# adaLN, multi-query attention and a bilinear FFN on one core: side products on one PSUM bank, one row half per key tile, and heads' outputs through DRAM

## The chip, the core and the metric

The kernel runs on one core of a Trainium2 chip. Time is device time in microseconds of one execution. The median before is 1765.92 us (three runs, 1764.85 to 1766.06). The engines are called PE (TensorE, matmuls), DVE (VectorE), ACT (ScalarE), POOL (GpSimd) and SP (SyncE, which issues the DMAs).

## The reference

```python
# x: 2048 x 512 (f32), 32 heads of 16, one key and one value head, F = 1792
mod = (silu(c) @ w_mod).reshape(1, 6, 1, 512)          # sa, ca, ga, sb, cb, gb
h = layernorm(x) * (1 + ca) + sa
q, k, v = h @ wq, h @ wk, h @ wv                       # k, v: 2048 x 16, shared by all heads
p = softmax(q k^T / 4)
x = x + ga * ((p v) @ wo)
h = layernorm(x) * (1 + cb) + sb
x = x + gb * (((h @ w_gate) * (h @ w_up)) @ w_down)
```

## The kernel before

**Units and key tiles.** The 2048 queries are cut into `NQ` = 8 blocks of 256, the 32 heads into four groups of 8: 32 units `u`, with `b, g = divmod(u, 4)`. A unit holds 16 key tiles of 128 keys, 512 key tiles in all. A key tile has two steps (`p` = 0, 1). Each operand is split into f16 halves (high and low part), so that a product has three terms; queries and keys are laid out so that one matmul over 48 to 50 rows holds all the terms of a score.

**The two row halves.** Scores need 50 of PE's 128 rows. So they are paired: one matmul on rows 0 to 63 (`a` = 0) and one on rows 64 to 127 (`a` = 1) run side by side.

- `max_mm` (L548): a matmul `mx` of queries by 512 keys, and a DVE reduction (L559) to the row maximum. Maxima run ahead of the scores by `LEAD` = 38 steps. Each unit's maxima are transposed (L571) and written into two more rows of the queries, so that the score comes out with its maximum taken off.
- `qk_exp` (L589): a score `sc` of 128 keys by 512 queries, and the exponential on ACT (L596) into a tile `P`.
- `pv` (L598): the previous key tile's four `P` parts against values, four column groups side by side in f32 (eight matmul records), into one bank. Values carry a column of ones, so that sums come along.

After a unit `pv_out` (L605) evacuates the bank and `normalise` (L618) divides by the sums through two small DRAM round trips; its `mult` leaves the heads' output as two f16 parts in `och`, of which four stand in SBUF.

**Side products.** Everything else that is dense is a `Group`: n products of 512 columns that accumulate in one bank, and an evacuation. `q_proj` has 12 products in a group, `wo_work` 12 (two groups for each block), gate and up 12 each (seven pairs for each block, each product as two of 256 columns), down 42 (two groups for each block). A block of queries has 24 + 168 + 84 = 276 products. `duo` (L483) takes two groups at a time, in the banks `misc` and `spare`: in its first turn group 0 has the upper rows and group 1 the lower ones, in its second turn the other way round, so that a bank is never written by both halves at once. While no duo runs, `spare` serves as a third bank for scores.

PSUM has eight banks: three `mx`, two `sc`, `misc`, `spare` and `pv`.

**The order.** The instructions of each engine stand in the order in which the Python loop writes them. In a key tile the loop writes for each step two pairs of `mx` and `sc`; between the steps come side products (as many as `pace` finds due, `burst`), after the second step the previous tile's `pv`. Evacuations are put into `posts` and written a step later. Block b's side work starts in block b + 1, at step 16 of its first unit. The last block's own side work comes after attention: `cover`, `run`.

**Weights.** From step 0 of attention on, `side_step` writes one item at a time: first every weight slice is loaded and squared on ACT (L873) and summed on POOL (L875) for bounds (`ABS_GAP` steps apart), then loaded again and split in f16 parts on POOL (`SPLIT_GAP` apart). `LAG` items lie between load and use.

Of the kernel before, what the change touches and what calls it, by code (L numbers as in the profile page):

```python
# [21 lines left out]
NB = 4  # L22
# [7 lines left out]
LEAD = 38  # L30
ABS_GAP = 1.5
SPLIT_GAP = 2.0
GC = 448
LAG = 3
NSC = 2
NMX = 3
PRE_FILL = 1000.0
# [19 lines left out]
def adaln_mqa_glu_kernel(ctx: ExitStack, tc: tile.TileContext, x_in, wq_in, wk_in, wv_in, wo_in,  # L57
# [43 lines left out]
    wqs = work.tile([128, KC, 128], F32, name="wqs", tag="xl", bufs=4)  # L101
# [3 lines left out]
    for i in range(6, 8):  # L105
        xts.append(work.tile([128, 2, D], F32, name="P", tag="P", bufs=4))
    for i in range(8):
        if i == 2:
# [5 lines left out]
           for tag, n in (("n2", 2), ("ev", 3), ("P", 4), ("P", 4))]  # L114
    for w in wq0:
        nc.gpsimd.memset(w, 0.0)
    wqst = [work.tile([128, D], F32, name="wqst", tag=("gf", "xl")[k // 2], bufs=(2, 4)[k // 2]) for k in range(KC)]
# [177 lines left out]
    mrow = work.tile([128, 256], F32, name="modrow", tag="xl", bufs=4)  # L295
# [181 lines left out]
    def product(p, g, i, j, rows, start, stop):  # L477
        left, right = g.op(i) if g.parts == 1 else g.op(i, j)
        w = 512 // g.parts
        nc.tensor.matmul(p[:, j * w:(j + 1) * w], left[rows], right[rows], start=start and j == 0,  # L480
                         stop=stop and j == g.parts - 1, skip_group_check=g.parts > 1)
# [68 lines left out]
    def max_mm(u, i, a):  # L550
# [3 lines left out]
        if i == 0 and a == 0:  # L554
            mparts[u] = work.tile([128, 2, 2, 4, 4], F32, name="mpart")
# [30 lines left out]
    och = {}  # L586
    rsum = {}

    def qk_exp(u, kt, p, a):  # L589
        s = sst[u % 3]  # L590
        if (u, kt, p) not in ptl:
            ptl[u, kt, p] = work.tile([128, 2, D], F32, name="P", tag="P", bufs=4)
        t = ps_sc()
        nc.tensor.matmul(t, kst[64 * a:64 * a + 50, kt * 128:(kt + 1) * 128],  # L594
                         s[64 * a:64 * a + 50, p, :], start=True, stop=True)
        nc.scalar.activation(ptl[u, kt, p][:, a, :], t, AF.Exp)  # L596

    def pv(u, kt):  # L598
        if kt == 0:
            pvb[u] = psum.tile([128, 512], F32, name="pv", tag="pv", bufs=1)  # L600
        for j in range(4):
            p, a = divmod(j, 2)
            nc.tensor.matmul(pvb[u][32 * j:32 * j + 32, :], vst[:, kt, :], ptl[u, kt, p][:, a, :],  # L603
# [14 lines left out]
    def normalise(u):  # L618
# [13 lines left out]
        def mult():  # L632
# [3 lines left out]
            h = work.tile([128, 2, QT], F16, name="och", tag="och", bufs=4)  # L636
# [17 lines left out]
    xls = {}  # L654
# [3 lines left out]
    def load_x(b, t):  # L658
        xl = work.tile([128, D], F32, name="xl", tag="xl", bufs=4)
        r0 = b * QT + t * 128  # L660
        nc.sync.dma_start(xl, x_rows[r0:r0 + 128, :])
        xls[b, t] = xl

    def wo_work(b):
# [13 lines left out]
        def fin(t):  # L678
            def f(p):
                if b < NQ - 1:  # L680
                    x1 = work.tile([128, D], F32, name="x1", tag="x1", bufs=4)
                else:
                    x1 = work.tile([128, D], F32, name="x1p", tag="P", bufs=4)
                nc.vector.scalar_tensor_tensor(x1, p, sca[:, 7:8], xls[b, t], op0=OP.mult, op1=OP.add)  # L684
                x1s[b, t] = x1
# [22 lines left out]
                if t == 1:  # L708
                    for j, d in enumerate((4, 6)):
                        after(d, n2f[b, j])  # L710
                    if tick[0] is not None:
                        turned.extend([tick[0] + 8 + 2 * j, *it[1:], b] for j, it in enumerate(ln2_work(b, ps_mx)))
# [9 lines left out]
    def ln2_work(b, bank=None):  # L722
# [3 lines left out]
        def tr(j):  # L726
            def f():
                if j == 0:
                    h2s[b] = big.tile([128, 2, KC, QT], F16, name="h2T", tag="h2T", bufs=2)
# [100 lines left out]
    def late_weights():  # L830
# [11 lines left out]
        def m1():  # L842
            st["row"] = work.tile([128, D], F32, name="modrow", tag="xl", bufs=4)
# [20 lines left out]
        def stage(n):  # L864
            t = work.tile([128, D], F32, name="wsl", tag="xl", bufs=4)
# [137 lines left out]
    later = {}  # L1003
    mstep = [0]

    def drain_posts():
        todo = posts[:]
        posts.clear()
        if tick[0] is not None:
            tick[0] += 1  # L1010
            todo += timers.pop(tick[0], [])
# [8 lines left out]

    def max_half(a):
        u, i = divmod(mstep[0], NSTEP)
        if a == 1:
            mstep[0] += 1
        if u >= NU:
            return
        max_mm(u, i, a)
        if a == 1 and u + 1 < NU and i == (QPRE if u else QPRE0):
            load_q(u + 1)
        if i == NSTEP - 1 and a == 1:  # L1030
            max_fin(u)
            (_, f, g), = max_rows(u)
            later[mstep[0] + 1] = (f, g)

    def late_max():
        for at in [m for m in later if m <= mstep[0]]:
            f, g = later.pop(at)
            f()
            posts.append(g)

    fill = deque()
    cur = {"gen": None, "left": 0, "swapped": -9, "wait": 0, "one": False}
    credit = [0.0]

    END = NU * NSTEP

    def pace(step):

        n, most = cur["left"], 0.0
        if n:
            most = n / max((cur["due"] - step) / 2, 1.0)
        for _, kind, what, due in fill:
            n += 4.0 if kind == "solo" else what.n if kind == "one" else 2 * what[0].n
            kept = RESERVE / PAIR if due > (NU - 1) * NSTEP else 0.0
            most = max(most, (n - kept) / max((due - step) / 2, 1.0))
        return most

    def open_gate(step):  # L1060
        if not fill or (fill[0][1] == "one" and step < cur["wait"]):
            return False
        if fill[0][1] == "duo" and NU * NSTEP - step < 2 * -(-fill[0][2][0].n // BURST) + 2:
            return False
        gate = fill[0][0]
        if len(gate) > 2 and ready[0] < gate[2]:
            return False
        if len(gate) > 3 and step < ln_end.get(gate[3], END) + LN_WAIT:
            return False
        if gate[0] is None:  # L1070
            gate[0] = step + gate[1]
        return gate[0] <= step

    def fill_gap(step):


        if cur["gen"] is None:
            if not open_gate(step):
                return
            _, kind, what, due = fill.popleft()  # L1080
            if kind == "solo":
                _, f, post = what
                credit[0] -= 4.0
                f()
                if post:
                    posts.append(post)
                return
            if kind == "one":
                cur.update(gen=plain(what), left=what.n, turn=what.n, second=True, due=due, swapped=-9, one=True)
            else:  # L1090
                begin(step, what, due)
        if cur["one"]:
            burst(step, max(1, min(int(credit[0]), cur["left"], MOST_ONE)))
            return
        turn = cur["turn"]
        parts = max(-(-turn // BURST), min(round(turn / max(credit[0], 1.0)), turn // LEAST), 1)
        n = -(-turn // parts)
        if not cur["second"]:
            n = max(n, -(-cur["turn"] // max((NU * NSTEP - 2 - step) // 2, 1)))
        burst(step, n)  # L1100

    def begin(step, two, due, tags=("misc", "spare")):
        cur.update(gen=duo(*two, tags=tags), left=2 * two[0].n, turn=two[0].n, second=False, due=due, swapped=-9,
                   one=False)

    def burst(step, n):
        for _ in range(n):
            swap = next(cur["gen"], None)
            credit[0] -= 1.0
            cur["left"] -= 1  # L1110
            cur["turn"] -= 1
# [173 lines left out]
```

## Time and profile before

| | us |
|---|---|
| median of the runs | 1765.92 |
| the profiled execution | 1765.83 |
| its span | 1764.0 |
| PE busy | 1700.3 |
| DVE busy | 1416.7 |
| ACT busy | 1252.3 |
| POOL busy | 472.9 |

The granted clock of PE was 0.99 on average. In the rows of the profile a group reads: line, engine, operation, tiles written and read, shapes, count, then busy time, mean ns of one, and idle time of the engine just before it with what ended most of that. In a timeline a row is: start, time until the last of the merged instructions ends, engine, line, operation, tiles, shapes, count and idle time. A window's row is: the window, its length, busy time and count of PE, PEld (weight loads), DVE, ACT and POOL, the granted clock, the DMA share and GB/s; where it was asked for one line's instructions, it holds their engine alone. PE's matmuls are pipelined and their ends are modelled: what a matmul costs is read from one start to the next.

### The profile page before, as it was taken

Reading aid. Unit: us, or ns where it says so; the run is one execution under the profiler, and the core shown is the slowest. Engines: PE = TensorE matmul, PEld = TensorE weight load, DVE = VectorE, ACT = ScalarE, POOL = GpSimd, SP = SyncE. Lnnn points to the kernel's source line nnn. Section 1 sums busy time; section 2 is a strip of 40 time slices with the busy share of each in tenths; the row PEclk is TensorE's granted clock in tenths of the full one; section 3 lists DMA queues with packets and bytes.
Section 4 is the critical chain, followed back from the end, with each engine's and each line's share of the span. In section 5 each row is a group of like instructions: output and inputs, shape, how many; then the busy total and the mean of one; then the engine's idle time right before and its main releaser. Section 6 shows DMA issues by size and latency. Waiting matters only on the chain.

```text
span 1764.0 us, 38680 instructions
## 1 busy us (share of the span) xinstructions
PE 1700.3 (96%) x15571; PEld 699.7 (40%) x15571; DVE 1416.7 (80%) x2367; ACT 1252.3 (71%) x2343; POOL 472.9 (27%) x711
## 2 busy tenths in 40 slices
PE   6999999889999999999999999999999999999999
PEld 3322222234433344334443344334443444334556
DVE  7788888878988889889888988889888888886021
ACT  3468887767777777777777777777777777777710
POOL 5724343788912011111112011201112011201112
PEclk9899999989999999999999999999999999999999
DMA  5223321322200000000000000000000000000000
GB/s 198 89 74 103 94 87 52 99 83 78 78 25 12 24 10 8 23 10 25 12 25 13 24 12 10 20 10 24 13 25 12 25 13 11 19 23 7 8 31 13
DMA packets 68735, 67.15 MB, mean 38 GB/s; under 512 B 24518, under 2 KB 53322, under 8 KB 68556
## 3 DMA queue, kind: packets, MB, share of 16 engines
q1 hardware_dynamic: 66972, 64.35, 11.9%
q8 instruction: 122, 2.00, 0.5%
q14 instruction: 57, 0.47, 0.1%
q10 hardware_dynamic: 1584, 0.33, 0.1%
HBM read 51.25 MB, written 8.92 MB: 34 GB/s over the span
## 4 chain that ended last, share of the span: by engine, by line
PE 82%; ACT 9%; DVE 4%; POOL 3%; issue 2%; SPq 0%; DMA 0%; ACTq 0%; DVEq 0%; POOLq 0%
PE pv L603 27%; PE misc L480 26%; PE mx L557 13%; PE sc L594 13%; ACT P L596 6%; DVE mpart L559 2%; ACT ev L609 1%; ACT hf L742 1%; PE misc L257 1%; PE mx L733 1%; DVE x L684 1%; ACT qf L524 0%; POOL ry L189 0%; DVE bs L223 0%; PE mxt L571 0%
## 5 line engine op out<-in xcount | busy, mean ns | idle before, releaser
L559 DVE TENSOR_REDUCE mpart<-mx 128x1 f32<-128x512 f32 x2048 | 1306.8, 683 | 193.0 <-PE sc L594 163.4
L596 ACT ACTIVATE P<-sc 128x512 f32<-128x512 f32 x2048 | 1108.4, 595 | 329.6 <-PE sc L594 326.1
L557 PE MATMUL mx<-kst,sst 48*128 48x512 f16 x2048 | 657.8, 383 | 11.4 <-DVE mpart L559 7.4
L594 PE MATMUL sc<-sst,kst 50*128 50x512 f16 x2048 | 638.7, 380 | 30.1 <-ACT P L596 18.0
L603 PE MATMUL pv<-P,vst 128*32 128x512 f32 x4096 | 548.3, 608 | 0.0
L557 PEld LDWEIGHTS <-sst 48*128 48x128 f16 x2048 | 163.3, 94 | 528.5 <-issue 484.1
L480 PE MATMUL misc<-h2T,wg 64*128 64x256 f16 (+1 forms) x2520 | 319.5, 269 | 1.3 <-DVE h2T L746 1.1
L480 PE MATMUL misc<-h2T,wu 64*128 64x256 f16 (+1 forms) x2520 | 319.2, 269 | 0.2 <-DVE x L804 0.2
L480 PEld LDWEIGHTS <-wu 64*128 64x128 f16 (+1 forms) x2520 | 237.0, 94 | 41.3
L480 PEld LDWEIGHTS <-wg 64*128 64x128 f16 (+1 forms) x2520 | 236.3, 94 | 38.4 <-issue 5.9
L594 PEld LDWEIGHTS <-kst 50*128 50x128 f16 x2048 | 149.7, 94 | 93.0 <-issue 69.9
L790 POOL TENSOR_SCALAR glu<-gf 128x512 f16<-128x512 f32 x56 | 34.7, 620 | 522.8 <-DVE gf L788 522.8
L480 PE MATMUL misc<-wd,glu 64*128 64x512 f16 (+1 forms) x1176 | 166.6, 376 | 0.4
L603 PEld LDWEIGHTS pv<-P,vst 128*32 128x32 f32 x4096 | 80.8, 108 | 146.1 <-issue 142.1
L635 POOL TENSOR_TENSOR oc<-oc,rr 128x256 f32<-128x256 f32 x31 | 22.6, 730 | 350.3 <-DMA sst<-qd 324.7
L480 PEld LDWEIGHTS <-glu 64*128 64x128 f16 (+1 forms) x1176 | 66.5, 94 | 81.3 <-issue 7.1
L788 DVE TENSOR_TENSOR gf<-misc,g 128x512 f32<-128x512 f32 x56 | 38.2, 683 | 71.9 <-ACT g L782 40.3
L875 POOL TENSOR_TENSOR kwb<-kwb,wsl 128x448 f32<-128x448 f32 (+1 forms) x40 | 47.6, 1191 | 84.3 <-ACT wsl L873 82.6
L791 POOL TENSOR_TENSOR glu<-gf,glu 128x512 f16<-128x512 f32 x56 | 64.8, 1156 | 4.7
L782 ACT ACTIVATE g<-misc 128x512 f32<-128x512 f32 x56 | 33.5, 598 | 37.3 <-PE misc L480 36.9
L480 PE MATMUL misc<-h,wq 64*128 64x512 f16 x384 | 52.4, 382 | 1.2 <-ACT qf L524 1.2
L480 PE MATMUL misc<-wo,och 64*128 64x512 f16 (+1 forms) x360 | 47.0, 375 | 0.0
(223 smaller groups left out, 703.4 us busy)
## 6 DMA issues: line engine op xcount, KB each, us to landing
wsl<-in_B_w_gate_dram SPq DMA_DIRECT2D x32, 224.0 KB
wsl<-in_B_w_up_dram SPq DMA_DIRECT2D x32, 224.0 KB
wsl<-in_B_w_down_dram SPq DMA_DIRECT2D x28, 256.0 KB
sst<-qd SPq DMA_DIRECT2D x372, 16.0 KB
qd<-q SPq DMA_DIRECT2D x16, 256.0 KB
oc<-ev SPq DMA_DIRECT2D x256, 16.0 KB
rr<-ri SPq DMA_DIRECT2D x32, 128.0 KB
xl<-in_A_x_dram SPq DMA_DIRECT2D x16, 256.0 KB
```

The lines of the kernel that those rows point to most:

```text
L480: nc.tensor.matmul(p[:, j * w:(j + 1) * w], left[rows], right[rows], start=start and j == 0, stop=stop and j == g.parts - 1, skip_group_ch ...
L557: nc.tensor.matmul(m, s[64 * a:64 * a + 48, p, t * 128:(t + 1) * 128], kst[64 * a:64 * a + 48, kc * 512:(kc + 1) * 512], start=True, stop= ...
L559: nc.vector.tensor_reduce(mparts[u][:, a, p, t, kc:kc + 1], m, axis=AX.X, op=OP.max)
L594: nc.tensor.matmul(t, kst[64 * a:64 * a + 50, kt * 128:(kt + 1) * 128], s[64 * a:64 * a + 50, p, :], start=True, stop=True)
L596: nc.scalar.activation(ptl[u, kt, p][:, a, :], t, AF.Exp)
L603: nc.tensor.matmul(pvb[u][32 * j:32 * j + 32, :], vst[:, kt, :], ptl[u, kt, p][:, a, :], start=(kt == 0), stop=(kt == KT - 1))
L635: eng.tensor_tensor(o, o, st["r"], op=OP.mult)
L782: nc.scalar.activation(st["g", f], p, AF.Copy, scale=2.0 ** -45)
L788: nc.vector.tensor_tensor(gf, p, st["g", f], op=OP.mult)
L790: nc.gpsimd.tensor_scalar(hi, gf, 1.0, 0.0, op0=OP.mult, op1=OP.add)
L791: nc.gpsimd.tensor_tensor(lo, gf, hi, op=OP.subtract)
L875: nc.gpsimd.tensor_tensor(acc, acc, t, op=OP.add)
```

## The change

**One bank, one half at a time.** A queue of single groups takes the place of duos and of `pace`. If a group is at hand, a pair of key tiles holds six of its products (`SIDE`): the even tile their upper row halves, the odd tile their lower ones. In a tile with such a half the other half does the maxima and scores: seven slots, in each of which one half has a side piece (the last: a score) and the other alternately an `mx` and an `sc`. So the tile of the upper half has four maxima and three scores of `a` = 1 and one score of `a` = 0, the next tile the reverse; `P` tiles are by half (`kt, a`) instead of by step, and have five buffers. A tile without a group at hand has the old four slots. All groups use `misc`, and `spare` is always a bank for scores.

The lower row half waits until the upper one is done, and the next upper half for that: the first piece gets a dependency on the exponential before last (`exps[-2]`), or, for gate and up groups when less than `LATE_FROM` = 126 groups are left, on a one-element POOL memset that itself depends on the last piece. In these tiles a slot has the `mx` or `sc` ahead of the piece.

**The queue.** Ten `q` groups, then for each block: `wo`, the down groups of the block before (for block 0 the two `q` groups left), gate and up; in the end the last down groups. An item starts only in an even tile. What is not done when attention ends comes after it. When the maxima have ended, 20 tiles before the scores do, a tile has its four scores and then six (`ENDING`) products over all 128 rows.

**DRAM.** Each unit's output goes to DRAM (`ohd`), and a block's four are read back (`load_o`) when its `wo` is near the head of the queue, from eight tiles after the block's end. The residual rows are loaded into `x1` and added to there.

**Numbers.** `LEAD` 38 to 40, `ABS_GAP` 1.5 to 2.0, `SPLIT_GAP` 2.0 to 2.4, `LAG` 3 to 2, `xl` buffers 4 to 3, `P` 4 to 5, one `h2T` instead of two.

PE, in attention, between two `pv` where gate and up products stand; before, a duo of gate (`wg`) and up (`wu`) behind the first step's pairs (`sst` are queries, `kst` keys):

```order
L557 LDWEIGHTS sst_123
L557 MATMUL mx<-kst,sst_123 128x512 [waits DVE_49]
L480 LDWEIGHTS wu
L480 MATMUL misc<-h2T,wu 128x256
L480 LDWEIGHTS wg
L480 MATMUL misc<-h2T,wg 128x256
L480 LDWEIGHTS wu
L480 MATMUL misc<-h2T,wu 128x256
```

and now, where a gate group begins behind a down group:

```order
L563 LDWEIGHTS sst_123
L563 MATMUL mx<-kst,sst_123 128x512 [waits DVE_49]
L615 MATMUL pv<-P,vst 32x512 x4
L563 LDWEIGHTS sst_123
L563 MATMUL mx<-kst,sst_123 128x512 [waits DVE_49]
L486 LDWEIGHTS wg [waits DVE_49]
L486 MATMUL misc<-h2T,wg 128x256 [waits Pool_49]
L486 LDWEIGHTS wg
L486 MATMUL misc<-h2T,wg 128x256
L606 LDWEIGHTS kst
L606 MATMUL sc<-sst_126,kst 128x512 [waits Activation_49]
```

Before, pieces of two groups alternate and do not wait; now pieces of one group alternate with maxima and scores, and the first piece of a group stands right behind the first `mx` after `pv` and waits for DVE, which empties the bank.

PE again, in the last key tiles, where no maxima are left. Before:

```order
L603 MATMUL pv<-P,vst 32x512 x4
L594 LDWEIGHTS kst
L594 MATMUL sc<-sst_124,kst 128x512 [waits Activation_49]
L594 LDWEIGHTS kst
L594 MATMUL sc<-sst_124,kst 128x512 [waits Activation_49]
L480 LDWEIGHTS wu
L480 MATMUL misc<-h2T,wu 128x256
```

and now:

```order
L606 LDWEIGHTS kst
L606 MATMUL sc<-sst_124,kst 128x512 [waits Activation_49]
L606 LDWEIGHTS kst
L606 MATMUL sc<-sst_124,kst 128x512 [waits Activation_49]
L606 LDWEIGHTS kst
L606 MATMUL sc<-sst_124,kst 128x512 [waits Activation_49]
L606 LDWEIGHTS kst
L606 MATMUL sc<-sst_124,kst 128x512 [waits Activation_49]
L486 LDWEIGHTS glu
L486 MATMUL misc<-wd,glu 128x512 [waits DVE_49]
```

The second pair of scores has moved from behind the side products to ahead of them. By count of the program, 360 products of side groups stand behind the last `pv` before, and 864 now; the transposes there (`n2` into `mx` or `misc`) are 8 before and 24 now.

The core of the diff:

```diff
     def qk_exp(u, kt, p, a):
         s = sst[u % 3]
-        if (u, kt, p) not in ptl:
-            ptl[u, kt, p] = work.tile([128, 2, D], F32, name="P", tag="P", bufs=4)
+        if (u, kt, a) not in ptl:
+            ptl[u, kt, a] = work.tile([128, 2, D], F32, name="P", tag="P", bufs=NP)
...
-            och[divmod(u, UB)] = h
+            ohd[u] = dram.tile([128, 2, QT], F16, name=f"oh{u}")
+            nc.sync.dma_start(ohd[u], h)
...
+    def piece(i, rows):
+        g = cur["g"]
+        for j in range(g.parts):
+            m = product(cur["p"], g, i, j, rows, i == 0 and rows.start == 0, i == g.n - 1 and rows.stop == 128)
+            if cur["after"] is not None:
+                tc.add_manual_dep(m.ins, cur["after"].ins.name, SYNC, reason="row halves of one bank in turn")
+                cur["after"] = None
+        cur["last"] = m
...
+    def advance(n):
+        cur["n"] += n
+        if cur["n"] == cur["g"].n:
+            posts.append(lambda g=cur["g"], p=cur["p"]: g.post(p))
+            cur["g"] = None
...
+    for k in range(NU * KT):
+        drain_posts()
+        spare["scores"] = not spare["held"]
...
+        ending = done["m"][0] >= NU * NSTEP
+        if k % 2 == 0:
+            turn = None
+            if cur["g"] is None and k and queue and queue[0].ok(k):
+                begin(queue.popleft())
+            if cur["g"] is not None and not ending:
+                turn = 0
+        slots = []
+        if ending:
+            slots = [[lambda: score_half(0), lambda: score_half(1)] for _ in range(2)]
+        elif turn is None:
+            for _ in range(2):
+                slots += [[lambda: max_half(0), lambda: score_half(1)], [lambda: score_half(0), lambda: max_half(1)]]
+        else:
+            few, many = turn, 1 - turn
+            n0, h = cur["n"], HALF[turn]
+            other = [lambda i=i: piece(n0 + i, h) for i in range(SIDE)] + [lambda: score_half(few)]
+            score = [(max_half, score_half)[i % 2] for i in range(SIDE + 1)]
+            late = cur["g"].parts > 1 and len(queue) < LATE_FROM
+            slots = [[o, lambda f=f: f(many)][::-1 if late else 1] for f, o in zip(score, other)]
+        for j, slot in enumerate(slots):
+            if j == (len(slots) + 1) // 2:
+                hooks(2 * k)
+                drain_mids()
+                drain_posts()
+            for f in slot:
+                f()
+        if ending:
+            for _ in range(ENDING):
...
+                piece(cur["n"], ALL)
+                advance(1)
+        if turn is not None:
+            cur["after"] = exps[-2]
+            if late:
+                cur["after"] = nc.gpsimd.memset(token, 0.0)
+                tc.add_manual_dep(cur["after"].ins, cur["last"].ins.name, SYNC, reason="end of a row half")
+            if turn == 1:
+                advance(SIDE)
+            turn = 1 - turn
+        if k:
+            u, kt = divmod(k - 1, KT)
+            pv(u, kt)
```

`hooks` writes the weight items and the steps of `normalise`; `max_half`, `score_half` and `product` issue one `mx`, one score or one row half of a product. Behind the loop the rest of the queue runs group by group over all 128 rows, with the banks of `misc`, `spare`, `mx` and `sc` in turn.

More of the change, by code (lines that the diff above doesn't have):

```diff
@@ L586, in adaln_mqa_glu_kernel, with load_o @@
     och = {}
+    ohd = {}
+    def load_o(b):
+        for ch in range(UB):
+            och[b, ch] = work.tile([128, 2, QT], F16, name="och", tag="och", bufs=4)
+            nc.sync.dma_start(och[b, ch], ohd[b * UB + ch])
     rsum = {}
@@ L864, in stage @@
         def stage(n):
-            t = work.tile([128, D], F32, name="wsl", tag="xl", bufs=4)
+            t = work.tile([128, D], F32, name="wsl", tag="xl", bufs=NXL)
             nc.sync.dma_start(t[:, :sl[n][3]], sl[n][2])
@@ L1038, in late_max @@
             f()
             posts.append(g)
[L1043 to L1106, printed above, removed]
+    lead_duo = {"gen": None}
+    def burst(n):
         for _ in range(n):
[L1108 to L1111, printed above, removed]
+            swap = next(lead_duo["gen"], None)
             if swap is None:
-                cur["gen"], cur["left"], cur["wait"] = None, 0, step + ONE_WAIT
-                return
-            if swap:
-                cur["turn"], cur["second"], cur["swapped"] = cur["left"], True, step
+                lead_duo["gen"] = None
+            if swap is not False:
@@ L1235, in adaln_mqa_glu_kernel @@
-    tail = deque(plain(g) for _, _, two, _ in fill for g in two)
-    def cover(budget):
-        while tail and budget > 0:
-            drain_posts()
-            if next(tail[0], None) is None:
-                tail.popleft()
-            budget -= 216
-        drain_posts()
-    def run(groups):
-        for g in groups:
-            for _ in plain(g):
-                pass
-    cover(6000 - 216 * left)
-    nrm = normalise(NU - 1)
-    nrm[0]()
-    cover(3000)
-    nrm[1]()
-    cover(5000)
@@ new lines, in adaln_mqa_glu_kernel @@
+    loaded = {}
+    ffn = [ffn_work(b) for b in range(NQ)]
+    queue = deque(Item(qs.popleft()) for _ in range(len(qs) - Q_LAST))
+    for b in range(NQ):
+        queue.extend(Item(g, weights=KC + 1, block=b) for g in wo_work(b))
+        if b:
+            queue.extend(Item(g, weights=len(slices)) for g in ffn[b - 1][1])
+        else:
+            queue.extend(Item(g) for g in qs)
+        queue.extend(Item(g, weights=slices_of(f) + 1, chain=b) for f, two in enumerate(ffn[b][0]) for g in two)
@@ L1266 @@
+    rest()
+    while queue:
+        for it in list(queue)[:3]:
+            if at[0] >= 20:
+                it.call(k + 8)
+        it = queue.popleft()
+        while it.block is not None and it.called is None or it.chain is not None and it.chain not in ln_end:
+            tail_tick()
+            if at[0] >= 20:
+                it.call(k + 8)
+        begin(it)
+        rest()
+    drain_posts()
 _INS = ["A_x", "A_wq", "A_wk", "A_wv", "A_wo", "B_w_gate", "B_w_up", "B_w_down", "c", "w_mod"]
```

249 lines of the change are left out of this document (124 added, 125 removed).

## The prediction

> **What bounds the kernel now.** I read the page first, then the windows of one block of queries, then the timelines of single key tiles on each engine. A key tile is the work between two starts of `pv`: four `mx`, four `sc`, the side products that stand there, and one `pv`.
>
> The first lines and the costliest groups of the page:
>
> ```profile
> span 1764.0 us, 38680 instructions
> PE 1700.3 (96%) x15571; PEld 699.7 (40%) x15571; DVE 1416.7 (80%) x2367; ACT 1252.3 (71%) x2343; POOL 472.9 (27%) x711
> L559 DVE TENSOR_REDUCE mpart<-mx 128x1 f32<-128x512 f32 x2048 | 1306.8, 683 | 193.0 <-PE sc L594 163.4
> L596 ACT ACTIVATE P<-sc 128x512 f32<-128x512 f32 x2048 | 1108.4, 595 | 329.6 <-PE sc L594 326.1
> L782 ACT ACTIVATE g<-misc 128x512 f32<-128x512 f32 x56 | 33.5, 598 | 37.3 <-PE misc L480 36.9
> L788 DVE TENSOR_TENSOR gf<-misc,g 128x512 f32<-128x512 f32 x56 | 38.2, 683 | 71.9 <-ACT g L782 40.3
> ```
>
> DVE and ACT wait for PE's scores (163.4 and 326.1 us), so PE sets the pace. Now the windows: from the first `pv` on, one steady block of 64 key tiles, and all that follows the last tile's start.
>
> ```profile
> 102.57:300.80 198.23, 183.42 (x1361) 55.38 (x1360) 168.77 (x284) 166.51 (x325) 70.21 (x69) 0.99 0.26 79
> 647.40:844.00 196.60, 195.35 (x1927) 81.09 (x1925) 172.98 (x284) 148.54 (x278) 27.10 (x46) 1.00 0.06 17
> 1676.80:1764.00 87.20, 80.77 (x548) 52.46 (x542) 14.54 (x25) 8.43 (x14) 16.32 (x30) 1.00 0.07 22
> ```
>
> A steady block takes 196.6 us, 3.07 us a tile, and holds a whole block's 276 side products (24 of `wo`, 168 gate and up, 84 down), 4.3 a tile. The early block has few side products and is no faster (198.2). Why is seen in one tile without any. PE first, then ACT and DVE (the DVE row is from a stretch in which it never waits):
>
> ```profile
> 155.22 0.39 PE L557 MATMUL mx<-kst,sst 48*128 48x512 f16 x1
> 155.23 0.60 PE L594 MATMUL sc<-sst,kst 50*128 50x512 f16 x2
> ...
> 156.33 0.86 PE L594 MATMUL sc<-sst,kst 50*128 50x512 f16 x2 [0.28 <-ACT P L596]
> 156.82 0.39 PE L557 MATMUL mx<-kst,sst 48*128 48x512 f16 x1
> 157.14 1.07 PE L603 MATMUL pv<-P,vst 128*32 128x512 f32 x8
> 158.14 0.39 PE L557 MATMUL mx<-kst,sst 48*128 48x512 f16 x1
> ```
>
> ```profile
> 155.68 1.08 ACT L596 ACTIVATE P<-sc 128x512 f32<-128x512 f32 x2 [0.39 <-PE sc L594]
> 156.65 0.58 ACT L873 ACTIVATE wsl<-wsl 128x448 f32<-128x448 f32 x1
> ```
>
> ```profile
> 95.43 7.86 DVE L559 TENSOR_REDUCE mpart<-mx 128x1 f32<-128x512 f32 x13 [0.16 <-PE mx L557]
> ```
>
> Only two banks take scores here. The score at 155.23 reaches ACT at 155.68 (0.45); the exponentials take 0.60 and follow each other by 0.49 (1.08 - 0.595); the third score goes out at 156.33, 0.05 after the first ends, and the fourth waits for the second: 0.45 + 0.49 + 0.60 + 0.05 = 1.59. Then 0.32 to `pv` and 1.00 for it: 2.91 us, the floor of every tile here. DVE needs 4 x 0.605 = 2.42 (7.86 / 13).
>
> **The change part by part.** *Slots.* Two row halves make a slot. A tile with four whole side products, and the two `pv` starts around one with six:
>
> ```profile
> 802.77 0.39 PE L557 MATMUL mx<-kst,sst 48*128 48x512 f16 x1
> ...
> 803.22 0.27 PE L480 MATMUL misc<-h2T,wg 64*128 64x256 f16 x1
> ...
> 804.09 0.38 PE L557 MATMUL mx<-kst,sst 48*128 48x512 f16 x1
> ...
> 804.69 1.06 PE L603 MATMUL pv<-P,vst 128*32 128x512 f32 x8
> 805.69 0.39 PE L557 MATMUL mx<-kst,sst 48*128 48x512 f16 x1
> ```
>
> ```profile
> 653.63 1.06 PE L603 MATMUL pv<-P,vst 128*32 128x512 f32 x8
> ...
> 656.91 0.64 PE L603 MATMUL pv<-P,vst 128*32 128x512 f32 x4
> ```
>
> Four products take 0.87, so a slot is 0.217; with the last slot's 0.32 to `pv` and 1.00 for it, n slots take (n - 1) x 0.217 + 1.32. Ten slots give 3.27; the rows give 3.28. The new tile has seven slots (six half products and a score on one half, four `mx` and three `sc` on the other): 2.62 us for three products' worth. The spare bank now always takes scores: the last score waits for the first exponential alone, 0.22 + 0.45 + 0.60 + 0.05 = 1.32 into the tile against its own 1.30. I take 2.62. It presumes that a half with two 256-wide pieces runs beside a 512-wide score though their starts no longer meet. The end of attention shows that:
>
> ```profile
> 1642.92 0.27 PE L480 MATMUL misc<-h2T,wg 64*128 64x256 f16 x1
> 1642.96 0.27 PE L480 MATMUL misc<-h2T,wu 64*128 64x256 f16 x1
> 1643.03 0.38 PE L594 MATMUL sc<-sst,kst 50*128 50x512 f16 x1
> 1643.07 0.27 PE L480 MATMUL misc<-h2T,wu 64*128 64x256 f16 x1
> ```
>
> With starts 0.04 apart each half still goes on after 0.11.
>
> *Hand-over of the bank.* Each new row half of a product waits: for the exponential before last, or, in the gate and up products from the second block on, for a GpSimd memset behind the last product. On PE every later score and `mx` stands behind that wait, on DVE and ACT the work on them. With exponentials 0.49 apart from 0.67 on, the third ends at 0.67 + 0.98 + 0.60 = 2.25; plus 0.05 it is 0.32 ahead of the next tile. The memset is bounded by the smallest POOL operations:
>
> ```profile
> L192 POOL TENSOR_SCALAR rt<-rt 128x1 f32<-128x1 f32 x16 | 3.1, 192 | 1.4
> ```
>
> The last half product starts near 1.19 and ends 0.27 later; 0.2 for the memset leaves it done by 1.8. Price 0, hidden under `pv`. The Trainium skill (TensorEngine Tiling, Restrictions and Gotchas) says that different row tiles cannot use one PSUM bank at the same time and that software must order them; no run so far shows what that order costs, and by the rows it costs nothing here.
>
> *One bank.* The next group starts in the tile after the last, behind the evacuation, and the evacuation stands behind the previous tile's work. For gate, ACT copies after four exponentials: the fourth starts at 2.15, the copy at 2.64, it ends 0.62 into the next tile, and PE loses about 0.62. For up, down and `wo`, DVE starts behind four reductions, 0.20 into the tile, takes 0.683, and PE loses 0.88. In before the next pair of groups starts behind `pv` and hides this. Nothing shows the wait itself: below it could be 0, if later work has slack of the same size; the order speaks for the full price. From key tile 76 to 491 there end 32 gate groups and 50 that DVE empties, and two `q`: 32 x 0.62 + 50 x 0.88 + 1.4 = 65 us.
>
> *Other groups:*
>
> ```profile
> L524 ACT ACTIVATE qf<-misc,qvs 128x512 f32<-128x512 f32 x16 | 11.0, 686 | 9.0 <-PE misc L480 4.7 <-PE mx L557 2.3 <-POOL q L526 2.1
> L571 PE MATMUL mxt<-ident,mm 128*16 128x128 f32 x32 | 8.9, 277 | 0.0
> L733 PE MATMUL mx<-ident,n 128*128 128x128 f32 x56 | 10.1, 308 | 0.0
> ```
>
> *The stages.* (a) Two more steps of maxima before attention, DVE-bound: 4 x 0.605; the first `pv` moves from 102.6 to 105.0. (b) 40 tiles with `q`: a square (0.58) now stands in the middle of every tile, the third exponential ends 0.49 later, 2.74, plus 0.05 is 2.80 a tile; each fourth ends in the `qf` copy, 2.64 + 0.49 + 0.69 + 0.05 = 3.87. Mean 3.07, 123 us. (c) 34 tiles without side work (`wo` waits for the heads until key tile 75): the floor is 1.10 + 1.32 = 2.42, as is DVE's with its reductions alone. Their share of the steady block:
>
> ```profile
> 647.40:844.00 196.60, 163.90 (x257) 1.00 0.06 17
> ```
>
> All DVE work there less this is 9.1 us, 0.14 a tile; a third of it, 0.05, does not come from side groups: 2.47 a tile, and the first ten still with their squares at 2.5, 84 us. (d) 416 tiles with side work: 416 x 2.62 = 1090, the 65 above, 40 transposes of the second norm at 0.31 (12), some 26 of row maxima at 0.28 (7). DVE's 2.42 + 0.14 stays under 2.62. (e) The last 20 tiles have no maxima. In before the pairs of scores lie on both sides of the products:
>
> ```profile
> 1643.48 1.07 PE L603 MATMUL pv<-P,vst 128*32 128x512 f32 x8
> 1644.48 0.47 PE L594 MATMUL sc<-sst,kst 50*128 50x512 f16 x2
> 1646.02 0.46 PE L594 MATMUL sc<-sst,kst 50*128 50x512 f16 x2
> 1646.41 0.64 PE L603 MATMUL pv<-P,vst 128*32 128x512 f32 x4
> ```
>
> That is 2.93. Now all four scores come first, and the fourth waits for an exponential, 1.10; then a slot, six full products and `pv`: 1.10 + 0.22 + 5 x 0.217 + 1.32 = 3.72, 74 us, and 1 for the last `pv`. The Trainium skill (TensorEngine Tiling, Key Properties) says that changing the tiling mode drains TensorE. The step of 0.32 to `pv` against a slot of 0.217 agrees, 0.10; full-height products add one such change a tile, so by the rule the sum would be 2 us longer.
>
> (f) After attention stand 864 products, 360 before. The price is that of the last ones now, 24 halves of 256 columns in 2.62 us, 0.218 each product:
>
> ```profile
> 1720.88 2.78 PE L480 MATMUL misc<-h2T,wg 128*128 128x256 f16 x24
> 1723.50 2.78 PE L480 MATMUL misc<-h2T,wu 128*128 128x256 f16 x24
> ```
>
> 504 x 0.217 = 109, and 16 more transposes, 5. Of the 87.2 us now 6.4 are PE idle behind the last block's chain; two other blocks now cover that. 87.2 + 109 + 5 - 6 = 195.
>
> (g) The DRAM round trip of the heads adds 32 writes and 32 reads on SP. A write waits on SP for POOL's three operations; behind it stand weight slices until about tile 105 and the next `q` loads. Two items of lead (two tiles, some 5 us) cover it; uncovered, six units at up to 2 us, 12. The reads have three tiles. The residual loads straight into `x1`, `P` with five buffers: nothing.
>
> Sum: 105 + 123 + 84 + 1090 + 65 + 12 + 7 + 74 + 1 + 195 = 1756 us of span (before 1764.0). The profiled execution took 1765.83 around it, 1.8 more, and the median of the runs is 1765.92. So 1758; with 1 us for what SP may lose, **1759**, 0.4% less. A measurement of this kernel tells 0.2% (3.5 us) from no change.
>
> The gain from attention is about 115 us (1462 us from first to last `pv`, with the last, against 1575), and nearly all goes back as 504 products after it.
>
> **The rivals.** *No stall at the groups' ends.* If evacuations are early enough, or PE catches up behind them, the 65 us shrink. For it: DVE and ACT have 0.1 to 0.6 us free in each tile. Against: in the program's order the copies stand behind the exponentials. Between half and all of it gone gives 1694 to 1727; I say 1715. *The hand-over shows.* If the wait of a row half ends after `pv`, PE stands still with all that feeds DVE and ACT, in each of 416 tiles, and the kernel is slower. It needs the third exponential to end 0.32 late, or POOL to be busy for 0.8 (its two `glu` operations follow each up group). Each 0.1 us beyond costs 42 us: 1801 at 0.1. Break-even is 0.02 us a tile. For it: seven slots leave ACT only that 0.32, and every stall delays the next exponential. *Only moved.* The work goes from one place to the other at the same price, and the time stays: that is inside my case, within 7 us of the sum.
>
> **How the numbers follow.** My case, 1740 to 1780, has 0.50: 0.28 of it under 1762, 0.10 within 3.5 us of before, 0.12 above. The stalls that vanish have 0.22, 1695 to 1740, all faster. The hand-over that shows has 0.28, 1780 to 1830, all slower. Faster 0.50, same 0.10, slower 0.40. 1705 to 1810 leaves out about 0.05 below and 0.12 above.
>
> **What would show it.** Right: tiles of 2.62 us inside a group, the first of a new group 0.6 (gate done) or 0.9 (up done) longer; tiles without side work at 2.4 to 2.5; 20 tiles of 3.7 at the end; about 195 us after the last `pv`. Wrong: seven-slot tiles at 2.75 or more with PE waiting on ACT or POOL at their first product (the hand-over), or a first product that never waits (no stall); a tail above 0.22 us a product.

## The result, and the profile after

The changed kernel takes 1804.38 us (median of four runs, 1803.31 to 1805.65), beside 1765.90 for the kernel before on the same chip: ratio 1.0219, 95% interval [1.0202, 1.0237]. It is slower by 38.5 us, where 0.4% faster was forecast; the time lies inside the range of the forecast, the sign is the other one. The profiled execution took 1803.31 us, its span 1801.5. The head of the page and two groups, of after:

```profile
span 1801.5 us, 37279 instructions
PE 1681.2 (93%) x14539; PEld 753.8 (42%) x14539; DVE 1392.7 (77%) x2367; ACT 1209.6 (67%) x2343; POOL 488.4 (27%) x911
L565 DVE TENSOR_REDUCE mpart<-mx 128x1 f32<-128x512 f32 x2048 | 1276.7, 681 | 141.6 <-PE mx L563 96.7
L563 PE MATMUL mx<-kst,sst 48*128 48x512 f16 x2048 | 765.4, 382 | 9.4 <-DVE mpart L565 6.7
```

PE still sets the pace: DVE's reductions wait for its `mx` (96.7 us), PE's `mx` hardly for DVE (6.7). But PE was busy 96% of the time and is now 93%. The lines of after that the following speaks of are L563 (`mx`), L606 (`sc`), L615 (`pv`), L486 (side products), L789 and L795 (the copies that empty a gate and an up group), L873 and L880 (load and square of a weight slice).

The five stages of both kernels, cut at the same key tiles: tiles 2 to 41, 42 to 75, 76 to 491, the last 20 with the last `pv`, and all behind its start. Before:

```profile
102.57:226.71 124.14, 114.41 (x844) 34.42 (x843) 104.24 (x172) 104.31 (x206) 42.75 (x43) 0.99 0.29 84
226.71:330.88 104.17, 96.06 (x708) 28.44 (x706) 89.89 (x157) 84.13 (x163) 49.36 (x59) 0.98 0.25 76
330.88:1616.60 1285.72, 1268.19 (x12377) 520.25 (x12375) 1122.98 (x1841) 966.08 (x1803) 290.30 (x444) 1.00 0.09 25
1616.60:1676.85 60.25, 59.07 (x655) 29.82 (x657) 7.80 (x14) 47.33 (x89) 10.65 (x13) 1.00 0.03 6
1676.85:1764.00 87.15, 80.72 (x548) 52.42 (x540) 14.54 (x25) 8.43 (x14) 16.32 (x30) 1.00 0.07 22
```

After:

```profile
104.58:235.82 131.24, 116.43 (x924) 38.93 (x923) 102.43 (x172) 105.82 (x209) 50.24 (x51) 0.94 0.29 89
235.82:332.47 96.65, 83.27 (x575) 20.72 (x573) 88.14 (x156) 78.73 (x157) 46.50 (x58) 0.96 0.28 82
332.47:1528.79 1196.32, 1141.07 (x10756) 501.89 (x10754) 1083.72 (x1812) 914.31 (x1782) 263.32 (x570) 1.00 0.10 29
1528.79:1605.87 77.08, 67.36 (x444) 23.05 (x445) 7.86 (x16) 46.39 (x90) 12.86 (x28) 1.00 0.07 20
1605.87:1801.52 195.65, 191.86 (x1404) 136.58 (x1396) 30.20 (x49) 22.59 (x38) 52.04 (x82) 1.00 0.08 25
```

The long middle stage gives 89.4 us and the second 7.5; the tail takes back 108.5, the last tiles 16.8, the first stage 7.1, and the start of attention 2.0. That is +37.5 of span. In the middle stage PE now stands idle for 1196.3 - 1141.1 = 55 us, where it had 17.5. Where it stands, the timeline shows. PE around the end of a gate group (key tile from 796.25) and of an up group (from 807.60):

```profile
796.25 1.07 PE L615 MATMUL pv<-P,vst 128*32 128x512 f32 x8
...
797.87 0.27 PE L486 MATMUL misc<-h2T,wu 64*128 64x256 f16 x1 [0.23 <-ACT g L789]
...
799.48 1.07 PE L615 MATMUL pv<-P,vst 128*32 128x512 f32 x8
...
804.97 1.07 PE L615 MATMUL pv<-P,vst 128*32 128x512 f32 x8
...
807.60 1.06 PE L615 MATMUL pv<-P,vst 128*32 128x512 f32 x8
809.53 0.39 PE L486 MATMUL misc<-wo,och 64*128 64x512 f16 x1 [0.86 <-DVE gf L795]
...
811.18 1.06 PE L615 MATMUL pv<-P,vst 128*32 128x512 f32 x8
```

A tile inside a group takes 2.63 us (804.97 to 807.60). The one behind a gate group takes 3.23, since its first piece waits for ACT's copy, and the one behind an up group 3.58, since the piece waits for DVE. Why DVE comes so late is in its own rows:

```profile
801.30 7.58 DVE L565 TENSOR_REDUCE mpart<-mx 128x1 f32<-128x512 f32 x12
808.80 0.68 DVE L795 TENSOR_TENSOR gf<-misc,g 128x512 f32<-128x512 f32 x1
```

The copy stands behind three tiles of reductions without a gap. The tile's first piece was due at 808.60, 1.00 behind `pv`; the copy starts 0.20 later, as forecast, lasts 0.68, and the piece starts 0.05 behind that.

### The profile page after: what moved, and what is told of

Same layout as the page of the kernel before. It is cut to its first block, busy times and chain, and to the rows that moved or that the text cites. A ratio compares the mean times of both kernels' runs of the same rounds, so it can differ in the third digit from the quotient of the medians.

```text
span 1801.5 us, 37279 instructions
## 1 busy us (share of the span) xinstructions
PE 1681.2 (93%) x14539; PEld 753.8 (42%) x14539; DVE 1392.7 (77%) x2367; ACT 1209.6 (67%) x2343; POOL 488.4 (27%) x911
## 4 chain that ended last, share of the span: by engine, by line
PE 73%; DVE 10%; ACT 10%; POOL 3%; issue 2%; SPq 1%; DMA 1%; ACTq 0%; POOLq 0%; DVEq 0%
PE misc L486 32%; PE pv L615 21%; PE sc L606 9%; PE mx L563 8%; ACT P L608 8%; DVE mpart L565 8%; DVE gf L795 1%; ACT g L789 1%; SPq L628 1%; ACT wsl L880 0%; PE mx L740 0%; ACT qf L530 0%; PE mxt L577 0%; DVE x L693 0%; DMA wsl<-in_B_w_gate_dram 0%
## 5 line engine op out<-in xcount | busy, mean ns | idle before, releaser
L565 DVE TENSOR_REDUCE mpart<-mx 128x1 f32<-128x512 f32 x2048 | 1276.7, 681 | 141.6 <-PE mx L563 96.7
L608 ACT ACTIVATE P<-sc 128x512 f32<-128x512 f32 x2048 | 1058.3, 602 | 320.6 <-PE sc L606 237.7
L563 PE MATMUL mx<-kst,sst 48*128 48x512 f16 x2048 | 765.4, 382 | 9.4 <-DVE mpart L565 6.7
L606 PE MATMUL sc<-sst,kst 50*128 50x512 f16 x2048 | 699.1, 380 | 33.1 <-ACT P L608 32.7
L615 PE MATMUL pv<-P,vst 128*32 128x512 f32 x4096 | 549.8, 609 | 0.0
L563 PEld LDWEIGHTS <-sst 48*128 48x128 f16 x2048 | 188.0, 94 | 303.4 <-issue 276.5
L486 PE MATMUL misc<-h2T,wg 64*128 64x256 f16 (+1 forms) x2112 | 257.5, 271 | 22.3 <-DVE gf L795 18.7
L486 PE MATMUL misc<-h2T,wu 64*128 64x256 f16 (+1 forms) x2112 | 256.4, 271 | 9.7 <-ACT g L789 9.7
L486 PE MATMUL misc<-wd,glu 64*128 64x512 f16 (+1 forms) x1008 | 239.8, 378 | 8.0 <-DVE x L693 4.1
L486 PEld LDWEIGHTS <-wg 64*128 64x128 f16 (+1 forms) x2112 | 190.4, 95 | 78.2 <-DVE gf L795 29.6
L486 PEld LDWEIGHTS <-wu 64*128 64x128 f16 (+1 forms) x2112 | 192.9, 95 | 64.9 <-issue 26.2
L606 PEld LDWEIGHTS <-kst 50*128 50x128 f16 x2048 | 182.6, 95 | 53.9 <-issue 25.2
L486 PEld LDWEIGHTS <-glu 64*128 64x128 f16 (+1 forms) x1008 | 87.7, 95 | 181.2 <-ACT P L608 69.6
L615 PEld LDWEIGHTS pv<-P,vst 128*32 128x32 f32 x4096 | 81.1, 108 | 146.4 <-issue 137.4
L795 DVE TENSOR_TENSOR gf<-misc,g 128x512 f32<-128x512 f32 x56 | 38.3, 685 | 134.0 <-PE misc L486 134.0
L789 ACT ACTIVATE g<-misc 128x512 f32<-128x512 f32 x56 | 34.5, 615 | 118.8 <-PE misc L486 98.5
L486 PE MATMUL misc<-h,wq 64*128 64x512 f16 x384 | 88.1, 391 | 9.8 <-ACT qf L530 8.6
L486 PE MATMUL misc<-wo,och 64*128 64x512 f16 (+1 forms) x312 | 75.1, 378 | 9.1 <-DVE x L693 5.1
```

The source lines that it names most:

```text
L486: return nc.tensor.matmul(p[:, j * w:(j + 1) * w], left[rows], right[rows], start=start and j == 0, stop=stop and j == g.parts - 1, skip_g ...
L563: nc.tensor.matmul(m, s[64 * a:64 * a + 48, p, t * 128:(t + 1) * 128], kst[64 * a:64 * a + 48, kc * 512:(kc + 1) * 512], start=True, stop= ...
L565: nc.vector.tensor_reduce(mparts[u][:, a, p, t, kc:kc + 1], m, axis=AX.X, op=OP.max)
L608: return nc.scalar.activation(ptl[u, kt, a][:, p, :], t, AF.Exp)
L789: nc.scalar.activation(st["g", f], p, AF.Copy, scale=2.0 ** -45)
L795: nc.vector.tensor_tensor(gf, p, st["g", f], op=OP.mult)
```

## The experiments

The times are medians; each ratio is to the kernel before, measured on the same chip, with its 95% interval.

**The group's copy written earlier.** The copy that empties the bank is written right behind the group's last piece, ahead of the last `mx` and `sc` of the tile.

```diff
             for f in slot:
                 f()
+            if turn == 1 and j == SIDE - 1 and n0 + SIDE == cur["g"].n:
+                cur["g"].post(cur["p"])
+                cur["posted"] = True
...
-            posts.append(lambda g=cur["g"], p=cur["p"]: g.post(p))
+            if not cur.pop("posted", False):
+                posts.append(lambda g=cur["g"], p=cur["p"]: g.post(p))
```

> A group's evacuation is written right behind its last piece, ahead of the last slot's exponential and reduction, so it needs one exponential or one reduction less to pass. One-bank theory (PE stands still at each group's end because the bank is emptied late): the first tile after a gate group falls from 3.23 us to about 2.8, after an up group from 3.56 to about 2.95, in all some 45 us, to about 1760. Hand-over theory (the waits between row halves are what costs): the same waits stand, so less than 5 us. Weights theory (late weight slices): no change.

Measured: 1752.63 us, ratio 0.9925 [0.9912, 0.9939], 51.8 below after and below the kernel before too. PE around the end of an up group (two groups ahead of the one above) and of the same gate group as above, then ACT and DVE:

```profile
763.18 1.07 PE L615 MATMUL pv<-P,vst 128*32 128x512 f32 x8
...
764.51 0.27 PE L486 MATMUL misc<-h2T,wg 64*128 64x256 f16 x1
...
766.12 1.06 PE L615 MATMUL pv<-P,vst 128*32 128x512 f32 x8
...
774.01 1.06 PE L615 MATMUL pv<-P,vst 128*32 128x512 f32 x8
...
776.75 1.06 PE L615 MATMUL pv<-P,vst 128*32 128x512 f32 x8
```

```profile
773.02 1.57 ACT L608 ACTIVATE P<-sc 128x512 f32<-128x512 f32 x3 [0.56 <-PE misc L486]
774.47 0.62 ACT L789 ACTIVATE g<-misc 128x512 f32<-128x512 f32 x1
774.95 1.36 ACT L608 ACTIVATE P<-sc 128x512 f32<-128x512 f32 x2
```

```profile
757.92 5.94 DVE L565 TENSOR_REDUCE mpart<-mx 128x1 f32<-128x512 f32 x9
763.77 0.68 DVE L795 TENSOR_TENSOR gf<-misc,g 128x512 f32<-128x512 f32 x1
```

ACT now copies behind the third exponential instead of the fourth, DVE behind one reduction less. The tile behind gate takes 2.74 (774.01 to 776.75) instead of 3.23, the one behind up 2.94 (763.18 to 766.12) instead of 3.56 for the same tile of after. Of the gain, 48.1 us lie in the middle stage (1148.25 us instead of 1196.32). The work and the banks are the same; only the place of the copy in two in-order queues has changed. So the stall at the groups' ends is real, it is set by that place, and the part that the earlier copy gives back is alone more than the whole loss of the change.

**The last scores split.** In the last 20 tiles the second pair of scores goes behind the six products, as before the change.

```diff
         if ending:
-            slots = [[lambda: score_half(0), lambda: score_half(1)] for _ in range(2)]
+            slots = [[lambda: score_half(0), lambda: score_half(1)]]
...
                 piece(cur["n"], ALL)
                 advance(1)
+            hooks(2 * k)
+            drain_mids()
+            drain_posts()
+            score_half(0)
+            score_half(1)
```

> In the last 20 key tiles the second pair of scores goes behind the six products again. If the fourth score's wait for an exponential is what makes them 3.8 us, they fall to about 3.1 and the kernel by some 12 us, to about 1792. If the change of tiling mode or the full-height products are the cost, they stay at 3.8.

Measured: 1789.90 us, ratio 1.0139 [1.0125, 1.0153], 14.5 below after. PE in one of these tiles, after and then this kernel:

```profile
1556.86 0.60 PE L606 MATMUL sc<-sst,kst 50*128 50x512 f16 x3
1557.93 0.37 PE L606 MATMUL sc<-sst,kst 50*128 50x512 f16 x1 [0.47 <-ACT P L608]
1558.23 1.48 PE L486 MATMUL misc<-h2T,wu 128*128 128x256 f16 x12
```

```profile
1551.18 0.39 PE L606 MATMUL sc<-sst,kst 50*128 50x512 f16 x2
1551.51 1.48 PE L486 MATMUL misc<-h2T,wu 128*128 128x256 f16 x12
1552.92 0.39 PE L606 MATMUL sc<-sst,kst 50*128 50x512 f16 x2
```

The wait of 0.47 us for an exponential is gone, and the two pairs each fit under the work between them: the 20 tiles take 62.1 us instead of 76.2, and every other stage stays within 1.3. With the second pair the writing of evacuations has moved too; but tiles with and without a group's end shorten alike, from 3.79 to 3.06 us.

**Weight slices earlier, with one `P` less, and with all five.** The first kernel loads the slices one item earlier (`LAG` 3, four `xl` buffers) and pays for the memory with a `P` buffer; the second frees it elsewhere (one `oh` buffer instead of two; an identity that nothing reads) and keeps `P` at five. The first kernel's edit, of which the second leaves out the last two lines:

```diff
-LAG = 2
-NXL = 3
+LAG = 3
+NXL = 4
...
-NP = 5
+NP = 4
```

> Three weight items of lead and four buffers as before, P with four buffers to make room. Weights theory (a slice lands after its square is due, ACT stands still, then PE): the three tiles of 6.5 to 6.7 us in the first 52 fall to below 4, some 12 to 20 us, to about 1788. One-bank theory alone: no change, and none from P with four buffers, since the buffer that a tile's second half takes is free by the end of the tile before.

> As the run with weights ahead, but P keeps its five buffers (one output buffer less and an unused constant dropped make the room). Weights theory: the 6.5 us tiles go and nothing takes their place, so 12 to 20 us less than the changed kernel, to about 1788. If P with four buffers was not what cost in that run: about 1815 again.

Measured: with four `P` 1815.25 us, ratio 1.0282 [1.0268, 1.0296], 10.9 above after; with five 1788.60, ratio 1.0126 [1.0106, 1.0146], 15.8 below after. What goes is a stall of after at three places, 16 tiles apart. SP, ACT and PE at the first of them, and the windows of that key tile and the two behind it, all of after:

```profile
153.18 5.00 SPq L628 DMA_DIRECT2D oc<-ev  x8
158.29 1.45 SPq L873 DMA_DIRECT2D wsl<-in_B_w_gate_dram  x1
```

```profile
162.31 0.58 ACT L880 ACTIVATE wsl<-wsl 128x448 f32<-128x448 f32 x1 [3.96 <-DMA wsl<-in_B_w_gate_dram]
```

```profile
163.43 0.58 PE L606 MATMUL sc<-sst,kst 50*128 50x512 f16 x1 [3.69 <-ACT P L608]
...
163.96 1.93 PE L615 MATMUL pv<-P,vst 128*32 128x512 f32 x8
```

```profile
157.26:163.96 6.70, 3.01 (x24) 0.87 (x22) 3.14 (x6) 2.74 (x7) 2.37 (x3) 0.96 0.46 144
163.96:167.93 3.97, 3.97 (x24) 1.02 (x22) 2.12 (x4) 2.30 (x5) 1.26 (x2) 0.64 0.26 73
167.93:170.60 2.67, 2.67 (x28) 0.91 (x28) 2.46 (x6) 2.57 (x7) 1.04 (x1) 1.00 0.03 3
```

Read from the top: at a unit's end SP issues eight DMAs of `pv_out` (`oc` from `ev`) in 5.00 us, the slice comes behind them, ACT stands 3.96 us at the square with the next exponentials queued behind it, and PE 3.69 us for a bank of scores. Then PE runs slowly: `pv` takes 1.93 us instead of 1.06, and the tile 3.97 at a granted clock of 0.64, beside 2.67 at 1.00. By finer windows the granted clock is 0.50 from 163.40 to 166.40. At the other two places PE stands 3.45 and 4.17 us, and the tiles behind (4.96 and 3.76 us) run at 0.50 throughout. The Trainium skill (TensorE: Matmul & The Clock Gate, HAM oscillation) says that idle gaps of PE above about 3.4 us drop its clock to half. The three waits and the 0.50 behind each agree. In the kernel with five `P` ACT's wait at this place has shrunk:

```profile
162.43 0.58 ACT L878 ACTIVATE wsl<-wsl 128x448 f32<-128x448 f32 x1 [1.00 <-DMA wsl<-in_B_w_gate_dram]
```

There the first two stages take 121.4 and 92.7 us, 13.9 less than in after, and the granted clock of the first is 0.98 instead of 0.94. The three stalled tiles and the few behind them (ten in all) account for it: they take 29.6 us instead of 43.6. With four `P` the late slices go too (126.9 and 93.9), but the middle stage takes 1216.5 instead of 1196.3. The fifth `P` buffer, which the expectation for that kernel took to cost nothing, is worth more than the slices (1788.60 beside 1815.25).

**A longer hand-over of the bank.** Three more one-element memsets in a chain between the last piece of a late row half and the first of the next.

```diff
                 tc.add_manual_dep(cur["after"].ins, cur["last"].ins.name, SYNC, reason="end of a row half")
+                for _ in range(3):
+                    cur["after"] = nc.gpsimd.memset(token, 0.0)
```

> Three more chained one-element memsets on POOL at each row half of the late gate and up groups, each some 0.27 us: the hand-over lands some 0.8 us later, 200 times. If it is hidden under pv with 0.8 us to spare, as the sum had it: under 10 us. Hand-over theory (it ends last): +0.8 us x 200, 160 us, to about 1960.

Measured: 1804.44 us, ratio 1.0220 [1.0206, 1.0234], the time of after. POOL:

```profile
806.41 0.09 POOL L1231 MEMSET token<- 1x1 f32 x1 [2.10 <-PE misc L486]
806.56 0.38 POOL L1234 MEMSET token<- 1x1 f32 x3
```

The last memset now ends 0.53 us behind the start of the first instead of 0.09, so the token comes 0.44 us later (0.8 was expected), and it costs nothing. Of the 200 tokens 150 have a product that depends on them; the one behind a group's last tile has none. Had the token been what PE waits for, that would have been 66 us. So the hand-over by the token is hidden. The one by the exponential before last this run leaves as it is; for the 416 tiles with side work the trace of after shows both. In 298 of them the first product starts 1.00 us behind `pv`, and in all others a new group begins or a transpose stands ahead. The forecast's rival of that name gave 1801 us, almost the time measured: a rival's time that comes true does not make its mechanism true. The Trainium skill (TensorEngine Tiling, Restrictions and Gotchas) has software order two row tiles on one bank; in these tiles that order is free.

**A second bank for side products, taken from the maxima.**

```diff
-NMX = 3
+NMX = 2
...
-    ring = {"tags": [("misc", 1)], "n": 0}
+    ring = {"tags": [("misc", 2)], "n": 0}
```

> Side groups get two banks, maxima two instead of three; all else as in the changed kernel. A group's evacuation then stands in nobody's way, 65 to 75 us less in attention. But the third and fourth maximum of a seven-slot tile wait for the first and second reduction: the fourth goes out at 1.03 + 0.68 + 0.05 = 1.76 instead of 1.30, so each tile takes 3.08 instead of 2.63. One-bank theory with three banks of maxima needed: 416 x 0.45 - 70, some 115 us slower than the changed kernel, about 1920. If the evacuations are the whole loss: about 1735.

Measured: 1945.48 us, ratio 1.1015 [1.0993, 1.1038], 141 above after. No group waits for its bank any more, but PE waits for `mx` banks. The group of `mx`, and DVE in one tile:

```profile
L565 PE MATMUL mx<-kst,sst 48*128 48x512 f16 x2048 | 765.9, 379 | 60.4 <-DVE mpart L567 28.5
```

```profile
745.81 2.48 DVE L567 TENSOR_REDUCE mpart<-mx 128x1 f32<-128x512 f32 x4 [0.60 <-PE misc L488]
```

Each tile takes 3.08 us: four reductions in a row, and 0.60 of DVE idle between, since two `mx` in stock do not carry it over `pv`. The third `mx` bank is worth more than the stall; the early copy of the first experiment needs no bank.

**The three mends together**, early copy, split scores, and slices earlier with five `P`:

> Early evacuation, split scores at the end, and weights ahead with five P buffers together. If the three losses are separate, they add up: 52 + 14 + 16 below the changed kernel, about 1722, and faster than before by 2.5%. If one hides another: 1735 to 1745.

Measured: 1723.46 us, ratio 0.9757 [0.9739, 0.9774], better than both kernels. It is 80.9 below after; the three alone give 51.8 + 14.5 + 15.8 = 82.1. The losses are separate and add up. Its middle stage and the last tiles:

```profile
318.19:1464.23 1146.04, 1133.44 (x10757) 500.74 (x10755) 1077.03 (x1813) 914.86 (x1782) 265.98 (x574) 1.00 0.11 31
1464.23:1527.02 62.79, 62.79 (x447) 24.77 (x445) 7.86 (x16) 48.08 (x90) 12.79 (x28) 1.00 0.09 25
```

In the middle stage PE is idle for 12.6 us instead of 55, in the last tiles not at all.

**Squares at the tile's end.** On top of the last kernel, the weight items of the first 55 tiles are written only at the end of a tile, never in its middle, where term (b) of the forecast had each square hold the third exponential.

```diff
-        side_step(step)
+        if step % 2 or step > 110:
+            side_step(step)
```

> As the three mends, and the weight items of the first 55 tiles go to the end of a key tile, behind its last exponential. Then the third exponential no longer ends 0.49 late. If the square in the middle holds up the next row half, the q tiles of 2.8 to 3.1 fall towards 2.65: some 5 to 8 us less than the three mends. Theory that the q tiles are held by ACT's total work: no change.

Measured: 1723.53 us, ratio 0.9753 [0.9735, 0.9771], no change; the first stage takes 117.7 us instead of 117.9. This doesn't speak against term (b), since the run moved few squares. Of the 36 squares in the 40 `q` tiles of after only six stand in the middle of a tile; the other 30 stand behind its fourth exponential, where this run wants them. ACT and PE of after, in a tile that follows a square of the first kind (`pv` at 111.83 and 114.63) and in one that follows a square of the second (133.76 and 136.39):

```profile
111.83 0.62 ACT L880 ACTIVATE wsl<-wsl 128x512 f32<-128x512 f32 x1
112.36 1.07 ACT L608 ACTIVATE P<-sc 128x512 f32<-128x512 f32 x2
...
134.71 0.60 ACT L880 ACTIVATE kwb<-wsl 128x448 f32<-128x448 f32 x1
135.40 2.07 ACT L608 ACTIVATE P<-sc 128x512 f32<-128x512 f32 x4
```

```profile
113.00 0.39 PE L486 MATMUL misc<-h,wq 64*128 64x512 f16 x1
...
134.76 0.39 PE L486 MATMUL misc<-h,wq 64*128 64x512 f16 x1
```

In the first, two exponentials follow the square. The former of them, on which the next row half depends, ends at 112.96 (112.36 and 0.60), and PE's first product starts at 113.00, 1.17 behind `pv` instead of 1.00: the tile takes 2.80. In the second, the product starts 1.00 behind `pv`, and the tile takes 2.63. Where this run did move squares, the tiles fell as term (b) says: two that take 2.80 and 2.79 in the kernel with three mends take 2.63 each. What that saves is under 2 us in all and was lost again in neighbouring tiles.

## Where the prediction held and where it failed

The step that failed is the sum for attention: stages priced at their floors plus the known stalls. Its terms (b) to (e) come to 1456 us (the 1462 given with the gain is not their sum), and attention took 1501.3 (104.6 to 1605.9; before 1574.3). The gain there was put at about 115 us, nearly all to be given back; it was 73. What is given back was right (108.5), so the sign was decided by the 45 us that are missing. No one term turned it. Late weight slices are 14, as the run with five `P` shows. The ends of groups are 9: right in kind, too small in size. Another 9 lie in tiles without side work and 16 are spread over the middle stage; both are read from the trace, and no run took them away. The last tiles add 2, and the rest of (b) and the transposes came out 4 below their price.

| term | forecast | after | what it was |
|---|---|---|---|
| (a) first `pv` | 105.0 | 104.6 | held |
| (b) 40 `q` tiles | 123 | 131.2 | late slices; 121.4 with them early, by luck |
| (c) 34 tiles without side work | 84 | 96.7 | late slices; 92.7 with them early |
| (d) 416 side tiles | 1174 | 1196.3 | group ends 74 instead of 65; others |
| (e) last 20 tiles, last `pv` | 75 | 77.1 | held; 3.8 us a tile for 3.72, as the step from the last score to the first full-height product is 0.30 (1557.93 to 1558.23), not 0.22 |
| (f) tail | 195 | 195.7 | held |
| sum | 1756 | 1801.5 | |

- **(g), the weights' lead.** Here the forecast's reasoning broke. It said that two items of lead, some 5 us, cover what stands ahead of a slice on SP, counted the heads' new transfers there, and put 1 us (12 uncovered). The eight DMAs of `pv_out`, which it did not count, hold SP for 5.00 us alone, and the slice itself came 4.0 behind its issue (158.29 to 162.31). They are no part of the change: SP's queue in before has them too (at 150.60, 5.01 us). But there the lead was three items. What the lost lead cost is what the run with five `P` gets back, 15.8 us, 14.0 of them at the three stalls.
- **(b).** The mechanism is right, the premise is not. A square in the middle makes the next tile 2.80 us (2.80 and 2.79 measured), and a group's end behind it 3.87 (3.90 and 3.85). But the forecast put a square into the middle of every tile, and only six of 36 stand there. Elsewhere a tile takes 2.63 or little more, and a group's end 3.39 to 3.44. That 121.4 us with early slices is near the forecast's 123 is luck: 30 tiles at 2.63 and ten at 3.4 would be 113, and the rest comes from longer tiles, some of them with row maxima, that had no term. What makes the others longer stays open.
- **(c).** With the slices early 19 of the 34 tiles take 2.47 us, as forecast, and 8.6 us more than forecast remain. 4.0 of them lie in tiles 57 to 62 (2.8 to 3.4 us), where the trace has the last steps of the weight bounds: column sums in an `mx` bank on PE, and small reductions that stand among DVE's maxima. 3.8 lie in tiles 42 to 52, with squares still running. The forecast had no term for the bounds. This is read from the trace and wasn't tried.
- **(d), the tile.** 2.63 us for 2.62. The two halves of a slot start within 0.01 us of each other (805.97 and 805.98), and the second 256-column piece runs beside the other half's matmul, as the end of attention in before had suggested. Some tiles of `wo` and down alternate between 2.63 and 2.68.
- **(d), the group ends.** The mechanism was right and the price low. By the intervals between `pv` starts, less 2.62: 32 tiles behind gate at 0.63 on average (forecast 0.62), 49 emptied by DVE at 1.06 (forecast 0.88), two behind `q` at 0.87. That is 20.2 + 51.9 + 1.7 = 74 us. Of the DVE ones, 0.05 is the step from the end of the copy to the matmul, which the forecast left out. The rival in which PE catches up behind the stall is refuted: none of the 416 tiles is shorter than 2.62, and the time came back only when the copy was written earlier.
- **Row maxima and transposes.** Row maxima cost 7.0 (forecast 7), transposes 9.6 (forecast 12). Some 16 us more of the middle stage are spread thin: 6 over tiles a few hundredths above 2.62, and 10 over single tiles, many in the first block, where POOL still splits weights (162.6 us for its 56 gate and up tiles, 159.2 to 160.7 in later blocks).
- **The hand-over** was priced at nothing, and is nothing in the 416 tiles; its rival is refuted there, though its time fits. It shows only where a square stands in the middle of a `q` tile, 0.17 us each, which is what term (b) forecast.

What would have warned: the steady block of before ran at 3.07 us a tile against its own floor of 2.91. Those 0.16 us over 490 tiles are 78 us. The forecast set floors plus known stalls for the new kernel against a measured time for the old one, and what that leaves out falls on one side only: here 45 us.

## What to carry to other kernels

With one accumulation bank, the place of the evacuation in the in-order queues of ACT and DVE is part of the critical path: write it right behind the last product, ahead of work that is not yet urgent (here 52 us of 1804). When a change pays with one big term for another, do not set floors on one side against measured time on the other; let what the kernel before needs above its own floor (here 78 us) widen the sum on its slow side. And before a prefetch is shortened, add up what stands ahead of it on its queue at the worst moment, not on average. Last, before a term is priced for every tile, look up in how many tiles the instruction really stands where the term has it (here six of 36).

## What the runs showed of the hardware

- A row half with two 256-column pieces, one behind the other, runs beside a half with one 512-column matmul: seven such slots with `pv` take 2.63 us, within 0.01 of what slots of 0.217 us, as measured in before, add up to.
- PE waits of 3.69, 3.45 and 4.17 us cost more than themselves: behind each the granted clock was 0.50, behind the first for 3.0 us, and that tile took 1.3 us longer than the next.
- Eight small DMAs keep their issuing queue for 5.00 us, 0.6 each, in both kernels, and a load behind them is that much later.
